# Stream lengths in steps of 16 columns, and a 96-byte shift of the tiles that TensorE streams

## The chip, the core and the metric

The kernel runs on one core of one Trainium2 chip. Its time is the device time of one execution in microseconds (us); of several runs the median is given. The hardware profiler records single executions: for each instruction a start and a duration, for TensorE the clock that it was granted, and for the DMA engines what they moved.

## What is computed

Two steps follow each other. The first is linear attention without a mask, for 8 batches of 8 heads, 576 positions and 64 features:

```python
kv  = einsum('bhsd,bhse->bhde', k, v)
out = einsum('bhsd,bhde->bhse', q, kv)
out = out / sqrt(mean(out * out, axis=-1) + 1e-6) * g_norm
```

Its result is read as 4608 tokens of 512 features. The second step is a mixture of 16 experts in 4 groups of 4. Each token chooses a group and then an expert of that group by the largest logit, is weighted with both softmax values, and passes through that expert alone:

```python
h  = maximum(x_of_expert @ w1[expert], 0)     # 512 -> 1024
ye = h @ w2[expert]                           # 1024 -> 512
out[tokens] = weight[:, None] * ye
```

## The kernel before

**Two stages.** In the first stage (to about 143 us) q, k and v are loaded, the products of attention and the logits of the router are made, and each token gets a place ("slot") in the list of its expert. The scaled rows of the tokens are kept in DRAM. In the second stage the experts are worked through in order of size, largest first, as 16 "regions" r = 0 to 15. The list `CAPS` (line 22) says how many slots a region has; it falls from 384 to 256. A region that had more tokens than slots would leave the rest to a loop at the end of the kernel, whose number of turns is computed on the device. Region 0 is done in the first stage and in the passage between the stages, in plain float32; the change doesn't touch its capacity.

**One region, r = 1 to 14.** The work is split so that float32 accuracy is kept while TensorE works on the type float32r. Each operand is written as a sum of a high and a low part: `xh`, `xl` for the tokens, `hh`, `hl` for the hidden layer, `whi`, `wlo` for the weights. A product is then three matmuls, high by high, low by high and high by low; `three` (lines 305 to 317) issues them, at lines 310, 311 and 315. In all regions but the last TensorE loads a 128 x 128 block of weights (LDWEIGHTS) and streams the tokens against it, so that the number of columns of each stream is the region's capacity:

- layer 1 (`layer1`): 8 blocks of features f, 4 blocks of the inner dimension, 3 matmuls each: 96 matmuls into the PSUM tiles `ps`, from `xh` and `xl`. After each f, ScalarE makes `hh` and VectorE `hl` (`split_h`, lines 284 and 285).
- layer 2 (`layer2_by_feature`): 4 blocks of output features d, 8 inner blocks, 3 matmuls each: 96 matmuls into the PSUM tiles `psy`, from `hh` and `hl`.

So a region is 192 matmuls, and regions 1 to 15 are 2880. Region 15 does its layer 2 the other way round (`layer2_by_token`): there the blocks of `hh` and `hl` are loaded, and 256 columns of `whi` or `wlo` are streamed.

**What runs beside it.** The order of instructions on each engine is the order in which they are written (a manual schedule). While region r is on TensorE, the loop over f issues the gather of the rows of region r + 2 (GpSimd queue, `gather`, line 1230), their scaling on GpSimd (`scale`), their way through DRAM (`put_x`, line 1242, and `get_x`, line 1248, on SyncE's queue), the weight loads of the next regions (line 212) and the scatter of region r - 1's result (`get_y`, `scatter_rows`). During layer 2 the function `side` splits the next region's w1 (lines 245 and 246) and turns and splits its tokens (`turn_x`, line 1253; `split_x`, lines 1262 and 1263). Sizes that go through DRAM in `put_x`, `get_x` and `put_y` are rounded up to 32 rows.

**Where the tiles lie.** Tiles of a pool are placed one behind the other in the order in which they first appear. `whi` and `wlo` are tiles of 8192 bytes per partition in the pool `big`, which lies first. The pool `moe` follows, in the order `xT`, `yq`, `yo3`, `xg`, `xq`, `xt`, the second weight tiles, `xh`, `xl`, `yo`, `hh`, `hl` and small ones. All these tiles but one, up to `hl`, are a multiple of 256 bytes long. The exception is `xg`, the gathered rows: 3 x 520 x 4 = 6240 bytes, which is 24 times 256 and 96 over. A block of weights starts 512 or 1024 bytes behind the last, a chunk of tokens 1536 bytes, so within the tiles nothing changes modulo 256. Modulo 256 bytes, every stream from `xh`, `xl`, `hh` or `hl` therefore starts 96 bytes behind the start of every weight block. In layer 2 of region 15, where the roles are exchanged, that is -96, or 160.

Of the kernel before, what the change touches and what calls it, by code (L numbers as in the profile page):

```python
# [9 lines left out]
F32 = mybir.dt.float32  # L10
# [8 lines left out]

CAPS = [384, 364, 354, 330, 326, 312, 302, 300, 292, 290, 284, 274, 268, 264, 260, 256]


GS = [8, 7, 5, 5, 7, 4]
# [32 lines left out]
def tile_linattn_moe(ctx: ExitStack, tc: tile.TileContext, qm, qt, k, v, router, w1, w2, out):  # L58
    nc = tc.nc
    P = 128  # L60
# [25 lines left out]
    RW = DM + H  # L86
# [70 lines left out]
    for r in range(NE):  # L157
        nc.gpsimd.memset(caps[:, r:r + 1], float(CAPS[r]))
    blk = cp.tile([P, 36], F32, name="blk")
# [88 lines left out]
    def blocks(cap):  # L248
        return [(j, min(P, cap - j * P)) for j in range((cap + P - 1) // P)]

    def gather_rows(xg, rows, idx, src=scr):
        return nc.gpsimd.indirect_dma_start(out=xg[0:rows, 0:RW], out_offset=None, in_=src,  # L252
                                            in_offset=bass.IndirectOffsetOnAxis(ap=idx[0:rows, :], axis=0))
# [20 lines left out]
    def scale_rows(eng, xg, out_=None):  # L274

        x = by_quarter(xg[:, 0:DM])
        out_ = x if out_ is None else by_chunk(out_)
        for h in range(2):
            hs = slice(2 * h, 2 * h + 2)
            d = eng.tensor_tensor(out=out_[:, hs], in0=x[:, hs], in1=factors(xg)[:, h], op=ALU.mult)  # L280
        return d
# [855 lines left out]
    with ExitStack() as ph:  # L1137
        mp = ph.enter_context(tc.tile_pool(name="moe", bufs=2))
# [87 lines left out]
        def quarter_rows(x, cap, a):  # L1226
            n = (cap + 31) // 32
            return x[0:32 * n, a * P:(a + 1) * P].rearrange("(b i) f -> i b f", i=32)

        def gather(r):  # L1230
            xg = mp.tile([P, 3, RW], F32, name="xg", bufs=1)
            for j, _ in blocks(CAPS[r]):
                st["gather"] = gather_rows(xg[:, j], P, gidx[:, r, j:j + 1])
            return xg

        def scale(r, g):
            for j, _ in blocks(CAPS[r]):
                scale_rows(nc.gpsimd, g[:, j])

        def put_x(r, g):  # L1240
            for j, rows in blocks(CAPS[r] + -CAPS[r] % 32):
                nc.sync.dma_start(xd[r % 2][j * P:j * P + rows, :], g[0:rows, j, 0:DM])

        def get_x(r):
            n = (CAPS[r] + 31) // 32
            xq = mp.tile([P, 12, P], F32, name="xq", bufs=1)
            for a in range(4):
                nc.sync.dma_start(xq[32 * a:32 * a + 32, 0:n, :], quarter_rows(xd[r % 2], CAPS[r], a))
            return xq, mp.tile([P, KC, 384], F32, name="xt", bufs=1)
# [80 lines left out]
        for i in range(2):  # L1330
            load_next(i)
        nxt = gather(1)
        gather_rows(xr, P, gidx[:, 0, 2:3])
        scatter_rows(st["ys"][:, 0, :], P, gidx0[:, 0:1])
# [5 lines left out]
        for i in range(2, 4):  # L1340
            load_next(i)
        nxt = gather(2)
        scale(2, nxt)
        left = ps_t.tile([P, 512], F32, name="left", tag="pst")
# [34 lines left out]
        for r in range(1, NE):  # L1379
# [10 lines left out]
            for f in range(FC):  # L1390
                if f in w2_at:
                    split_piece(w2c, w2_at[f], r in MOVED)
                ps = ps_h.tile([P, 512], F32, name="ps")
                layer1(ps[:, 0:cap], w1c, f, xh[:, :, 0:cap], xl[:, :, 0:cap])
                split_h(hh[:, f, 0:cap], hl[:, f, 0:cap], ps[:, 0:cap])
                if r > 1:
                    next(tables, None)
                    next(tables, None)
                elif f < len(psys):
                    nc.vector.memset(psys[f][:, DM // 2:384], 0.0)  # L1400
                if f == 0:
                    nxt2 = gather(r + 2) if r + 2 < NE else None
                if nxt2 and f == 1:
                    scale(r + 2, nxt2)
                if f >= 1:
                    next(turns, None)
                if todo and todo[0] in MOVED and f == 2:
                    results = get_y(*todo)
                if nxt and f in (1, 3):
                    load_next((f + 3) // 2)  # L1410
                if nxt2 and f == 4:
                    put_x(r + 2, nxt2)
                if f >= 5 and results:
                    scatter_rows(*results.pop(0))
                if f == FC - 1 and r + 1 == NE:
                    nc.gpsimd.drain()
# [26 lines left out]
    with ExitStack() as ph:  # L1443
# [4 lines left out]
        with tc.For_i(0, nv, 1) as it:  # L1448
# [19 lines left out]
            xg = op.tile([P, RW], F32, name="xgo")  # L1468
# [90 lines left out]
```

## Time and profile before

| | us |
|---|---|
| median of 3 runs | 572.38 |
| lowest and highest of the runs | 571.86, 573.12 |
| the profiled execution's own time | 569.92 |
| its span, from the first instruction to the last | 568.2 |

Rows of the profile name the line of the kernel, the engine, the operation, the tile written and the tiles read. PE is a matmul on TensorE, PEld the load of its weights, DVE is VectorE, ACT is ScalarE, POOL is GpSimd, SP is SyncE. Matmuls overlap: a matmul's recorded duration is the time from its start until its last column is out, and the next one starts long before that. What a matmul costs in a dense sequence is the time from its start to the next one's start, called its pitch here. A window from the first matmul of a region to the first of the next, divided by 192, is the region's mean pitch.

### The profile page before, as it was taken

The numbers are of one execution on the slowest core, as the hardware profiler recorded it, in microseconds if no ns is written. First come the engines' busy times: TensorE is split into PE (matmuls) and PEld (weight loads), VectorE is DVE, ScalarE is ACT, GpSimd is POOL, SyncE is SP. The second block draws the span as 40 slices with busy tenths as digits, with TensorE's granted clock in tenths as the row PEclk, the third lists the DMA queues.
The fourth block names the chain that finished last, engine by engine and source line by source line (L and its number), as shares of the span: only waits on it lengthen the run. The fifth ranks groups of instructions, "written<-read, shape, count | busy, mean of one in ns | idle before, by whom it ended". The sixth has DMA issues, their size and how long they took to land.

```text
span 568.2 us, 11528 instructions
## 1 busy us (share of the span) xinstructions
PE 545.6 (96%) x4335; PEld 523.7 (92%) x4335; DVE 376.8 (66%) x777; ACT 268.5 (47%) x530; POOL 208.9 (37%) x278
## 2 busy tenths in 40 slices
PE   8999988799989999999999999999999999999995
PEld 4789877588879999999999999999999999999995
DVE  4236988772467686676767676777767677877850
ACT  0367764621444344444545445454546455555540
POOL 4014433143461525152352434343526263630321
PEclk9999998999999999999999999999999999999998
DMA  9999999487979998899988999999999999799730
GB/s 268 371 413 376 365 363 397 153 312 247 276 282 323 281 344 222 262 318 294 303 248 300 260 323 262 316 266 319 299 307 282 300 320 320 273 279 306 253 116 33
DMA packets 77359, 164.06 MB, mean 289 GB/s; under 512 B 7979, under 2 KB 46075, under 8 KB 66293
## 3 DMA queue, kind: packets, MB, share of 16 engines
q1 hardware_dynamic: 69331, 141.14, 77.2%
q0 software_dynamic: 7824, 22.11, 13.2%
q8 instruction: 35, 0.57, 0.4%
q10 hardware_dynamic: 146, 0.04, 0.1%
q14 instruction: 23, 0.19, 0.1%
HBM read 125.82 MB, written 37.96 MB: 288 GB/s over the span
## 4 chain that ended last, share of the span: by engine, by line
PE 77%; DMA 13%; issue 3%; DVE 2%; ACT 2%; POOL 1%; SPq 1%; POOLq 0%; DVEq 0%; ACTq 0%
PE psy L310 11%; PE psy L315 11%; PE psy L311 11%; PE ps L311 11%; PE ps L315 11%; PE ps L310 11%; DMA m_v<-in_v_dram 3%; DMA m_q<-in_qm_dram 3%; PE l L299 3%; DMA m_k<-in_k_dram 3%; PE ops L515 2%; DMA scr<-xo 2%; PE kps L477 2%; PE ps L299 1%; DMA xs<-scr,sidx 1%
## 5 line engine op out<-in xcount | busy, mean ns | idle before, releaser
L246 DVE TENSOR_TENSOR wlo<-wr,whi 128x1024 fp32r<-128x1024 f32 (+1 forms) x172 | 155.2, 928 | 25.1 <-ACT whi L245 22.9
L310 PE MATMUL ps<-xh,whi 128*128 128x364 f32 (+14 forms) x480 | 144.9, 302 | 1.0 <-ACT xh L1262 1.0
L311 PE MATMUL ps<-xl,whi 128*128 128x364 f32 (+14 forms) x480 | 144.8, 302 | 0.4 <-DVE xl L1263 0.4
L315 PE MATMUL ps<-xh,wlo 128*128 128x364 f32 (+14 forms) x480 | 144.4, 301 | 0.0
L311 PE MATMUL psy<-hl,whi 128*128 128x364 f32 (+13 forms) x448 | 135.4, 302 | 0.0
L315 PE MATMUL psy<-hh,wlo 128*128 128x364 f32 (+13 forms) x448 | 135.4, 302 | 0.0
L310 PE MATMUL psy<-hh,whi 128*128 128x364 f32 (+13 forms) x448 | 135.3, 302 | 0.0
L245 ACT CAST whi<-wr 128x1024 fp32r<-128x1024 f32 (+1 forms) x172 | 127.9, 783 | 0.0
L284 ACT ACTIVATE hh<-ps 128x364 fp32r<-128x364 f32 (+14 forms) x120 | 50.5, 421 | 149.6 <-PE ps L315 148.5
L256 POOL DMA_INDIRECT out_dram<-yo,gall x45 | 55.5, 1234 | 110.9 <-DMA yo<-yd 90.4
L285 DVE SCALAR_TENSOR_TENSOR hl<-ps,hh 128x364 fp32r<-128x364 f32 (+14 forms) x120 | 55.9, 466 | 59.5 <-ACT hh L284 59.4
L310 PEld LDWEIGHTS ps<-xh,whi 128*128 128x128 f32 x480 | 90.8, 189 | 1.7 <-ACT xh L1262 1.6
L311 PEld LDWEIGHTS ps<-xl,whi 128*128 128x128 f32 x480 | 90.5, 189 | 1.2 <-DVE xl L1263 1.1
L280 POOL TENSOR_TENSOR xg<-xg 128x256 f32<-128x256 f32 x82 | 61.1, 770 | 80.4 <-DMA xg<-scr,gall 80.4
L315 PEld LDWEIGHTS ps<-xh,wlo 128*128 128x128 f32 x480 | 90.7, 189 | 0.0
L310 PEld LDWEIGHTS psy<-hh,whi 128*128 128x128 f32 x448 | 84.7, 189 | 0.0
L315 PEld LDWEIGHTS psy<-hh,wlo 128*128 128x128 f32 x448 | 84.6, 189 | 0.0
L311 PEld LDWEIGHTS psy<-hl,whi 128*128 128x128 f32 x448 | 84.5, 189 | 0.0
L252 POOL DMA_INDIRECT xg<-scr,gall x44 | 47.5, 1079 | 76.1 <-DMA xd<-xg 60.8
L1262 ACT ACTIVATE xh<-xt,rw 128x364 fp32r<-128x364 f32 (+14 forms) x60 | 32.5, 543 | 45.4 <-DVE xt L1253 45.4
L1315 DVE STREAM_TRANSPOSE yq<-psy 128x320 f32<-128x320 f32 (+3 forms) x52 | 26.7, 514 | 29.9 <-PE psy L315 29.8
L515 PE MATMUL ops<-kvx,m_q 128*128 128x168 f32 x256 | 42.0, 312 | 1.1 <-ACT xr L466 0.6
(254 smaller groups left out, 593.6 us busy)
## 6 DMA issues: line engine op xcount, KB each, us to landing
wr<-in_w_dram SPq DMA_DIRECT2D x64, 1024.0 KB, 9.2
scr<-xo SPq DMA_DIRECT2D x36, 256.0 KB, 9.1
m_q<-in_qm_dram SPq DMA_DIRECT2D x8, 1024.0 KB
xd<-xg SPq DMA_DIRECT2D x32, 256.0 KB, 5.7
m_k<-in_k_dram SPq DMA_DIRECT2D x7, 1024.0 KB, 8.3
m_v<-in_v_dram SPq DMA_DIRECT2D x7, 1024.0 KB
yo<-yd SPq DMA_DIRECT2D x26, 256.0 KB, 3.9
xq<-xd SPq DMA_DIRECT2D x20, 160.0 KB, 8.6
```

What stands on the lines that cost most here:

```text
L245: nc.scalar.copy(out=hi, in_=x)
L246: nc.vector.tensor_tensor(out=lo, in0=x, in1=hi.bitcast(F32), op=ALU.subtract)
L252: return nc.gpsimd.indirect_dma_start(out=xg[0:rows, 0:RW], out_offset=None, in_=src, in_offset=bass.IndirectOffsetOnAxis(ap=idx[0:rows, : ...
L256: sc = nc.gpsimd.indirect_dma_start(out=out, out_offset=bass.IndirectOffsetOnAxis(ap=idx[0:rows, :], axis=0), in_=yo[0:rows, :], in_offset ...
L280: d = eng.tensor_tensor(out=out_[:, hs], in0=x[:, hs], in1=factors(xg)[:, h], op=ALU.mult)
L284: nc.scalar.activation(out=hh, in_=ps, func=AF.Relu)
L285: nc.vector.scalar_tensor_tensor(out=hl, in0=ps, scalar=0.0, in1=hh.bitcast(F32), op0=ALU.max, op1=ALU.subtract)
L310: nc.tensor.matmul(ps, lhsT=stat_h(c), rhs=mov_h(c), start=(c == 0), stop=False)
L311: nc.tensor.matmul(ps, lhsT=stat_h(c), rhs=mov_l(c), start=False, stop=False)
L315: nc.tensor.matmul(ps, lhsT=stat_l(d), rhs=mov_h(d), start=False, stop=(d == n - 1))
L515: nc.tensor.matmul(o, lhsT=raw["q", b].rearrange("p j f -> p (j f)")[:, (pr * NJ + j) * P:(pr * NJ + j + 1) * P], rhs=kvx[b % 4][:, pr], s ...
L1262: nc.scalar.activation(out=xh, in_=x, func=AF.Copy, scale=g2[:, 0:1])
```

## The change

The capacities are raised to the next multiple of 16, and `xg` gets 24 more floats, which nothing reads or writes, so that all tiles behind it move by 96 bytes. The streams then start 192 bytes behind the weight blocks, modulo 256; in layer 2 of region 15 it is 64.

```diff
-CAPS = [384, 364, 354, 330, 326, 312, 302, 300, 292, 290, 284, 274, 268, 264, 260, 256]
+CAPS = [384, 368, 368, 336, 336, 320, 304, 304, 304, 304, 288, 288, 272, 272, 272, 256]
...
         def gather(r):
-            xg = mp.tile([P, 3, RW], F32, name="xg", bufs=1)
+
+
+            xg = mp.tile([P, 3 * RW + 24], F32, name="xg", bufs=1)[:, 0:3 * RW].rearrange("p (j f) -> p j f", j=3)
             for j, _ in blocks(CAPS[r]):
                 st["gather"] = gather_rows(xg[:, j], P, gidx[:, r, j:j + 1])
             return xg
```

## Rows read from the trace of the kernel before

**Rows 1.** The page: busy time, clock in 40 slices, chain that ended last.

```profile
PE 545.6 (96%) x4335; PEld 523.7 (92%) x4335; DVE 376.8 (66%) x777; ACT 268.5 (47%) x530; POOL 208.9 (37%) x278
PEclk9999998999999999999999999999999999999998
PE 77%; DMA 13%; issue 3%; DVE 2%; ACT 2%; POOL 1%; SPq 1%; POOLq 0%; DVEq 0%; ACTq 0%
```

**Rows 2.** Windows of single regions: capacities 364, 354, 302, 300, 292, 290, 268, 264, 260, 256.

```profile
core 0: us, PE busy (x) PEld busy (x) DVE busy (x) ACT busy (x) POOL busy (x), PEclk, DMA share, GB/s
158.92:193.91 34.99, 33.56 (x194) 32.18 (x193) 22.65 (x39) 16.79 (x31) 13.54 (x17) 1.00 0.93 294
193.91:225.90 31.99, 31.99 (x194) 31.99 (x194) 24.75 (x48) 13.70 (x24) 13.44 (x17) 1.00 0.98 291
...
312.19:339.07 26.88, 26.88 (x194) 26.88 (x193) 19.03 (x32) 13.27 (x24) 11.18 (x12) 1.00 1.02 297
339.07:365.94 26.87, 26.87 (x194) 26.87 (x193) 19.00 (x32) 13.22 (x24) 11.58 (x12) 1.00 0.97 293
365.94:391.35 25.41, 25.41 (x195) 25.41 (x193) 18.95 (x32) 13.15 (x24) 10.45 (x11) 1.00 0.98 295
391.35:417.59 26.24, 26.24 (x195) 26.24 (x193) 18.82 (x32) 13.11 (x24) 9.35 (x12) 1.00 1.01 308
...
467.72:492.53 24.81, 24.81 (x206) 24.73 (x205) 19.03 (x35) 14.33 (x27) 11.70 (x12) 1.00 0.91 281
492.53:515.88 23.35, 23.35 (x194) 23.35 (x193) 18.14 (x32) 12.85 (x24) 8.30 (x10) 1.00 0.99 302
515.88:538.92 23.04, 23.04 (x194) 23.04 (x193) 17.57 (x32) 12.73 (x23) 4.23 (x3) 1.00 0.92 289
538.92:561.84 22.92, 22.92 (x194) 22.87 (x192) 8.39 (x13) 7.03 (x14) 4.96 (x5) 1.00 0.28 86
```

**Rows 3.** The same windows with TensorE alone: the sum over regions 1 to 15.

```profile
sum 402.92, PE 401.49; mean PE 26.77
```

**Rows 4.** Timeline of the first matmuls at capacity 302: start us, us, engine, line, operation.

```profile
312.19 0.30 PE L310 MATMUL ps<-xh,whi 128*128 128x302 f32 x1
312.19 0.19 PEld L311 LDWEIGHTS ps<-xl,whi 128*128 128x128 f32 x1
312.33 0.30 PE L311 MATMUL ps<-xl,whi 128*128 128x302 f32 x1
312.33 0.19 PEld L315 LDWEIGHTS ps<-xh,wlo 128*128 128x128 f32 x1
312.47 0.30 PE L315 MATMUL ps<-xh,wlo 128*128 128x302 f32 x1
```

**Rows 5.** Timeline between the stages: 16 plain float32 matmuls of 256 columns, merged.

```profile
139.80 3.62 PE L303 MATMUL left<-wr,h 128*128 128x256 f32 x16
```

**Rows 6.** Matmuls by line and form: busy us, mean duration ns, idle before.

```profile
L310 PE MATMUL psy<-hh,whi 128*128 128x364 f32 x32 | 10.5, 329 | 0.0
...
L310 PE MATMUL psy<-hh,whi 128*128 128x292 f32 x32 | 9.5, 296 | 0.0
L311 PE MATMUL psy<-hl,whi 128*128 128x292 f32 x32 | 9.5, 296 | 0.0
...
L315 PE MATMUL psy<-hh,wlo 128*128 128x292 f32 x32 | 9.3, 292 | 0.0
...
L303 PE MATMUL left<-wr,h 128*128 128x256 f32 x16 | 3.6, 379 | 0.0
```

**Rows 7.** Timeline of VectorE in layer 2 at capacity 264: its last split of tokens.

```profile
513.63 0.45 DVE L1263 SCALAR_TENSOR_TENSOR xl<-xt,rw,xh 128x260 fp32r<-128x260 f32 x1
514.00 1.22 DVE L246 TENSOR_TENSOR wlo<-wr,whi 128x1024 fp32r<-128x1024 f32 x1
```

**Rows 8.** VectorE's split of the hidden layer in the windows of capacities 302 and 264.

```profile
L285 DVE SCALAR_TENSOR_TENSOR hl<-ps,hh 128x302 fp32r<-128x302 f32 x8 | 3.8, 470 | 4.8 <-ACT hh L284 4.8
...
L285 DVE SCALAR_TENSOR_TENSOR hl<-ps,hh 128x264 fp32r<-128x264 f32 x8 | 3.4, 429 | 3.1 <-ACT hh L284 3.1
```

## The prediction

> **What bounds the kernel now.** I first read the page [rows 1]: TensorE is busy for 96% of the span, it makes up 77% of the chain that ended last, and its granted clock is at the upper level (2.4 GHz) in nearly every slice. A busy TensorE need not be one at its peak, so the second view is the table of windows, one per region [rows 2]. From capacity 354 on, TensorE has no idle time in a region, and VectorE is the next at 19 of 27 us. So in this stage the end is set by the pitch of the matmuls, and by nothing that ends a wait. The windows of regions 1 to 15 add up to 402.9 us [rows 3], out of 568.2.
>
> The third step compares the pitch with the columns. In the timeline [rows 4] matmuls of 302 columns start 140 ns apart, and so does the window: 26.88 us / 192 = 140.0. One column per tick of 2.4 GHz would be 302 / 2.4 = 125.8 ns, so 14.2 ns per matmul are something else, called the excess. It isn't a matter of the column count: capacity 290 takes 26.24 us and capacity 292 only 25.41 [rows 2]. Per matmul that is 136.7 and 132.3 ns, an excess of 15.8 and 10.7. Capacity 354 has 166.6 - 147.5 = 19.1, and 302 and 300 take the same time. Nor is it a fixed cost of an instruction: plain float32 matmuls of 256 columns, between the stages, start (3.62 - 0.379) / 15 = 216.1 ns apart [rows 5, 6]; this form takes two ticks per column, 213.3 ns, so its excess is 2.7 ns, although it too loads weights for each matmul.
>
> What goes on during a float32r stream: the weights of the next matmul are loaded, from the same start on, for 190 ns [rows 4]. Stream and load read the same memory side by side, the stream at one word per tick without slack. My reading is that they meet in some part of the memory at times, and that the stream then waits; the half-rate stream has slack and doesn't. Where two address sequences meet depends on their distance and on where each stream begins and ends, which fits an excess that changes with two columns more or less.
>
> **What the change does to TensorE.** It adds columns: the capacities of regions 1 to 15 sum to 4476 before and 4592 after. 116 columns x 192 matmuls / 2.4 GHz = 9.3 us, all on the path, since TensorE is never idle there. This is sure, whatever else happens.
>
> It may remove excess. From the 402.9 us I take the stalls of the first region: its matmuls of 329 ns [rows 6] less 162.4 (the mean duration of the three kinds at capacity 292, 294.7, less its pitch of 132.3) are a pitch of 167, so 192 of them are 32.0 to 32.1 us of the 34.99 [rows 2], and 2.9 are stalls. I also take 1.4 us for the 12 transposes in the window of capacity 268 (206 instructions instead of 194). 398.6 us remain. The columns are 4476 x 192 / 2.4 = 358.1 us, so the excess is 40.5 us, 14.1 ns for each of 2880 matmuls. The change breaks even where the new excess is 14.1 - 9.3 / 2.88 = 10.9 ns.
>
> No row shows a stream of a multiple of 16 columns at a distance of 192 bytes, so I bound it. From below, 2.7 ns, the half-rate stream. From above, 14.1, the present mean, with one row near that: capacity 256 is a multiple of 16, at the old distance of 96 bytes (160 in its layer 2), and has 22.92 / 192 = 119.4 ns, an excess of 12.7 [rows 2]. It shows that a multiple of 16 alone isn't enough. Between them stand the best kinds of matmul that a region has: at capacity 292 the third kind lasts 292 ns where the others last 296 [rows 6], a pitch of 129.6 and an excess of 8. There identical shapes alternate between better and worse meetings, because the stream's end falls on another place each time. With all streams a whole number of 64-byte pieces, starting at a multiple of 64 from the weights, every matmul of all regions would meet its load in the same way. I take this to be a good meeting, and for its excess the middle between the floor (2.7) and the best kind that still has odd ends (8): 5.3 ns. Then regions 1 to 15 take 367.4 + 2880 x 5.3 ns = 382.6 us instead of 398.6, **16.0 us less**.
>
> **What lies beside it.** VectorE and ScalarE work on more columns: (470 - 429) / 38 = 1.1 ns per column in the split of the hidden layer [rows 8], some 0.1 us in a region, and hidden, as VectorE has 5 to 8 us to spare in each [rows 2]. If regions become shorter, the latest thing that TensorE needs is the last `xl`: at capacity 264 it ends at 514.08 [rows 7], 1.8 us before the next region starts at 515.88 [rows 2]; layer 2 would become at most 96 x 5.6 ns = 0.5 us shorter there even at the floor (116.0 against 121.6 ns), so the cover holds. The w1 piece behind it is needed only by the last feature blocks. On the queues nothing moves: rounded up to 32, all capacities give the sizes of before, so `put_x`, `get_x` and `put_y` and the transposes move the same bytes, and the gathers have the same three blocks; `get_y` and the scatters carry 116 rows more in all, off the path. The 24 floats of `xg` are never touched. I cost all of this at nothing. The DMA engines show a busy share near 1 [rows 2]; they move 281 to 308 GB/s in the middle regions, and a region that is 6% shorter would ask for as much more. A load that then comes late is the point where this cover could fail.
>
> **The rivals.**
>
> *The excess goes entirely* (2.7 ns): 367.4 + 7.8 = 375.2 us, 23.4 less, 549.0. For it: the half-rate stream reaches this floor with the same loads beside it. Against it: no float32r row does.
>
> *The meeting is a fixed one, but a bad one.* Today the excess varies and averages out; after the change one relation holds for all 2880 matmuls. Capacities 302 and 260 sit at one pitch, with 14.2 and 120.0 - 108.3 = 11.7 ns [rows 2]. If the new relation is like that of capacity 256, 12.7 ns, the stage takes 367.4 + 36.6 = 404.0 us, 5.4 more: 577.8. It decides from 10.9 ns upwards.
>
> *Addresses don't matter.* If the excess came from issuing or from the array, it would stay at 14.1 ns and only the columns would count: 581.7. Against it stand capacities 290 and 292. The Trainium skill ("SBUF — State Buffer", section "Who interferes with whom") says that TensorE has two independent read ports, one for the moving operand and one for the weights, and never waits on anyone; by that rule the shift can bring nothing and this rival holds. The float32r rows with 10 to 19 ns over one tick per column speak against it, but they don't show the reason.
>
> *The shift isn't where the diff says* (tiles placed in another way), or excess and columns cancel: within 1.1 us of before.
>
> *Another limit takes over*: late weights or rows give back half of the gain, some 564.
>
> **The numbers.** The sum was made on the profiled execution, 569.92 us with a span of 568.2; the median of the runs lies 2.5 higher, at 572.38. I subtract from the median: 572.4 - 16.0 = **556.4 us**. Chances: the forecast with its neighbours (3.5 to 10 ns) 0.45, no excess left 0.23, another limit 0.02, nothing measurable 0.06, bad meeting 0.14, addresses without effect 0.10. So faster by over 0.2% (about what a measurement of this kernel can tell from no change) 0.70, within 0.2% 0.06, slower 0.24. The range goes from the floor, less the scatter of runs, to the bad meeting: 547 to 578; it leaves out the last rival.
>
> **What would show it.** If I am right, the window of capacity 304 is 192 x (126.7 + 5.3) = 25.3 us, three kinds of matmul last alike, and equal capacities (four regions of 304) take equal times. The stage's windows add up to some 387. If the windows of 304 are 26.6 us or more (an excess of 12), the meeting is bad or addresses don't matter; capacity 256, whose columns are unchanged, tells those two apart: its 22.92 us change only if the distance matters. A new idle time of TensorE inside a region, with a DMA or `xl` as its end, would be the other limit.

## The result, and the profile of the changed kernel

The changed kernel takes **576.61 us** (median of 7 runs, 574.99 to 578.31), against 571.60 for the kernel before on the same occasions (7 runs, 568.81 to 573.12): a ratio of 1.0095 [1.007, 1.012], **slower by about 5 us**. The forecast was 556.4; the range, up to 578, holds it. The profiled execution took 574.99 us, 5.07 more than that of before.

The page of the changed kernel, answering to [rows 1]:

```profile
span 573.3 us, 11529 instructions
PE 552.1 (96%) x4335; PEld 529.7 (92%) x4335; DVE 384.3 (67%) x777; ACT 269.6 (47%) x530; POOL 211.8 (37%) x278
PEclk9999998799999999999999999999999999999998
PE 77%; DMA 13%; issue 3%; DVE 2%; ACT 2%; SPq 1%; POOL 1%; POOLq 0%; DVEq 0%; ACTq 0%
```

The same 4335 matmuls, the same share, the same chain: nothing has taken TensorE's place as the bound. The windows, answering to [rows 2, 3], are of regions with capacity 368, 304 (twice), 288, 272 (twice) and 256; the last line sums all 15:

```profile
core 0: us, PE busy (x) PEld busy (x) DVE busy (x) ACT busy (x) POOL busy (x), PEclk, DMA share, GB/s
194.53:226.96 32.43, 32.43 (x194) 32.43 (x193) 25.86 (x48) 13.81 (x24) 16.00 (x18) 1.00 0.95 289
...
340.62:367.25 26.63, 26.63 (x195) 26.63 (x193) 19.41 (x32) 13.27 (x24) 13.96 (x14) 1.00 0.96 298
367.25:393.87 26.62, 26.62 (x195) 26.62 (x193) 19.01 (x32) 13.28 (x24) 9.68 (x11) 1.00 1.02 302
...
420.50:446.09 25.59, 25.59 (x194) 25.59 (x193) 18.73 (x32) 13.02 (x23) 11.23 (x12) 1.00 1.00 313
...
471.69:496.72 25.03, 25.03 (x207) 24.98 (x205) 19.72 (x35) 14.40 (x27) 12.93 (x14) 1.00 0.87 289
496.72:520.40 23.68, 23.68 (x195) 23.68 (x193) 18.38 (x32) 12.96 (x24) 4.86 (x6) 1.00 0.94 294
...
544.08:566.69 22.61, 22.61 (x194) 22.57 (x192) 8.39 (x13) 7.01 (x14) 4.48 (x4) 1.00 0.28 85
sum 407.56, PE 406.10 PEld 404.57 DVE 290.28 ACT 197.19 POOL 156.05; mean PE 27.07 PEld 26.97 DVE 19.35 ACT 13.15 POOL 10.40
```

The stage takes 407.56 - 402.92 = 4.64 us more [rows 3], which is nearly all of the 5.07. The columns alone are worth 9.28, so the change has won back 4.64 elsewhere. Each window over 192 gives the pitch, and that less columns / 2.4 GHz the excess: 168.9 ns and 15.6 at capacity 368, 138.7 and 12.0 at 304, 133.3 and 13.3 at 288, 123.3 and 10.0 at 272, 117.8 and 11.1 at 256. Over all 2880 matmuls, without the first region's stalls (2.97 us; 2.91 before) and the 12 transposes in the window of one of the regions of 272 (1.35 us, as before), the excess is 35.9 us, 12.5 ns for each, where it was 14.1. The forecast wanted 5.3.

The three kinds of matmul last alike now, where [rows 6] had 296, 296 and 292 at capacity 292:

```profile
L315 PE MATMUL psy<-hh,wlo 128*128 128x304 f32 x128 | 38.5, 301 | 0.0
L311 PE MATMUL psy<-hl,whi 128*128 128x304 f32 x128 | 38.5, 301 | 0.0
L310 PE MATMUL psy<-hh,whi 128*128 128x304 f32 x128 | 38.5, 301 | 0.0
```

But that is a mean. The starts in the trace show that single pitches still wander, in a cycle; eleven in a row, in ns:

```
after, capacity 304:   140 136 137 142 139 139 137 136 143 138 139
before, capacity 292:  133 131 133 134 129 133 134 130 133 134 129
```

### The profile page after: what moved, and what is told of

It is laid out like the page before. It is cut to its first block, busy times and chain, and to the rows that moved or that the text cites. A ratio compares the mean times of both kernels' runs of the same rounds, so it can differ in the third digit from the quotient of the medians.

```text
span 573.3 us, 11529 instructions
## 1 busy us (share of the span) xinstructions
PE 552.1 (96%) x4335; PEld 529.7 (92%) x4335; DVE 384.3 (67%) x777; ACT 269.6 (47%) x530; POOL 211.8 (37%) x278
## 4 chain that ended last, share of the span: by engine, by line
PE 77%; DMA 13%; issue 3%; DVE 2%; ACT 2%; SPq 1%; POOL 1%; POOLq 0%; DVEq 0%; ACTq 0%
PE psy L311 11%; PE psy L315 11%; PE psy L310 11%; PE ps L311 11%; PE ps L315 11%; PE ps L310 11%; DMA m_v<-in_v_dram 3%; DMA m_q<-in_qm_dram 3%; PE l L299 3%; DMA m_k<-in_k_dram 2%; PE ops L515 2%; DMA scr<-xo 2%; PE kps L477 2%; PE ps L299 1%; DMA xg<-scr,gall 1%
## 5 line engine op out<-in xcount | busy, mean ns | idle before, releaser
L310 PE MATMUL ps<-xh,whi 128*128 128x304 f32 (+6 forms) x480 | 145.8, 304 | 1.0 <-ACT xh L1264 1.0
L311 PE MATMUL ps<-xl,whi 128*128 128x304 f32 (+6 forms) x480 | 145.6, 303 | 0.4 <-DVE xl L1265 0.4
L315 PE MATMUL ps<-xh,wlo 128*128 128x304 f32 (+6 forms) x480 | 145.2, 303 | 0.0
L311 PE MATMUL psy<-hl,whi 128*128 128x304 f32 (+5 forms) x448 | 136.3, 304 | 0.0
L315 PE MATMUL psy<-hh,wlo 128*128 128x304 f32 (+5 forms) x448 | 136.3, 304 | 0.0
L310 PE MATMUL psy<-hh,whi 128*128 128x304 f32 (+5 forms) x448 | 136.1, 304 | 0.0
L284 ACT ACTIVATE hh<-ps 128x304 fp32r<-128x304 f32 (+6 forms) x120 | 51.2, 427 | 152.5 <-PE ps L315 146.2
L256 POOL DMA_INDIRECT out_dram<-yo,gall x45 | 49.1, 1092 | 130.1 <-DMA yo<-yd 86.0
L285 DVE SCALAR_TENSOR_TENSOR hl<-ps,hh 128x304 fp32r<-128x304 f32 (+6 forms) x120 | 56.9, 474 | 57.8 <-ACT hh L284 55.2
L1264 ACT ACTIVATE xh<-xt,rw 128x304 fp32r<-128x304 f32 (+6 forms) x60 | 32.9, 550 | 45.6 <-DVE xt L1255 44.1
L1317 DVE STREAM_TRANSPOSE yq<-psy 128x320 f32<-128x320 f32 (+3 forms) x52 | 26.6, 512 | 28.7 <-PE psy L315 26.5
```

Source lines behind the costliest of these rows:

```text
L256: sc = nc.gpsimd.indirect_dma_start(out=out, out_offset=bass.IndirectOffsetOnAxis(ap=idx[0:rows, :], axis=0), in_=yo[0:rows, :], in_offset ...
L284: nc.scalar.activation(out=hh, in_=ps, func=AF.Relu)
L285: nc.vector.scalar_tensor_tensor(out=hl, in0=ps, scalar=0.0, in1=hh.bitcast(F32), op0=ALU.max, op1=ALU.subtract)
L310: nc.tensor.matmul(ps, lhsT=stat_h(c), rhs=mov_h(c), start=(c == 0), stop=False)
L311: nc.tensor.matmul(ps, lhsT=stat_h(c), rhs=mov_l(c), start=False, stop=False)
L315: nc.tensor.matmul(ps, lhsT=stat_l(d), rhs=mov_h(d), start=False, stop=(d == n - 1))
```

## The experiments

Theory A: the excess depends on the distance of the stream from the weights, together with the length. Theory B: on the length alone. Theory C: other engines and the DMAs slow the streams. Each excess below is a mean pitch less columns / 2.4 GHz.

**The two halves of the change by themselves.** The capacities without the 24 floats of `xg`, and the 24 floats with the old capacities:

```diff
-CAPS = [384, 364, 354, 330, 326, 312, 302, 300, 292, 290, 284, 274, 268, 264, 260, 256]
+CAPS = [384, 368, 368, 336, 336, 320, 304, 304, 304, 304, 288, 288, 272, 272, 272, 256]
```

> The raised capacities without the shift: streams stay 96 bytes behind the weights. Columns cost 9.3 us. Theory A: the excess differs from that of the whole change (12.3 ns on average), so the time differs from the whole change's 576.6 by more than 2 us either way. Theory B: the time of the whole change, within 1 us, as the shift does nothing.

```diff
-            xg = mp.tile([P, 3, RW], F32, name="xg", bufs=1)
+            xg = mp.tile([P, 3 * RW + 24], F32, name="xg", bufs=1)[:, 0:3 * RW].rearrange("p (j f) -> p j f", j=3)
```

> The shift alone, with the old capacities: streams 192 bytes behind the weights. No column is added. Theory A: windows of the regions change by some per cent, some up, some down; a time between 565 and 580. Theory B: nothing changes, within 1 us of the kernel before, region by region within 0.1 us.

The capacities alone took 581.02 us, a ratio to before of 1.0175 [1.0139, 1.0211]; the shift alone 570.23, 0.9966 [0.9936, 0.9997]. Windows of the capacities alone (one of 336, one of 304, one of 272, and 256):

```profile
227.10:256.55 29.45, 29.45 (x194) 29.45 (x194) 22.99 (x48) 13.60 (x24) 11.58 (x14) 1.00 0.92 287
...
341.35:368.55 27.20, 27.20 (x195) 27.20 (x194) 18.57 (x32) 13.27 (x24) 9.98 (x12) 1.00 0.90 282
...
499.77:524.09 24.32, 24.32 (x194) 24.32 (x193) 18.56 (x33) 12.96 (x24) 5.33 (x7) 1.00 1.01 316
...
548.41:571.19 22.78, 22.78 (x194) 22.73 (x192) 8.39 (x13) 6.99 (x14) 4.62 (x4) 1.00 0.29 85
sum 412.05, PE 410.45 PEld 408.91 DVE 287.41 ACT 197.13 POOL 151.31; mean PE 27.36 PEld 27.26 DVE 19.16 ACT 13.14 POOL 10.09
```

And of the shift alone (capacities 300, 292, 256):

```profile
341.00:367.24 26.24, 26.24 (x194) 26.24 (x193) 19.97 (x32) 13.21 (x24) 11.61 (x12) 1.00 0.99 306
367.24:393.48 26.24, 26.24 (x194) 26.24 (x193) 19.29 (x32) 13.15 (x24) 11.60 (x11) 1.00 1.01 311
...
541.20:562.97 21.77, 21.77 (x194) 21.73 (x192) 8.39 (x13) 7.00 (x14) 4.03 (x4) 1.00 0.29 88
sum 400.80, PE 399.17 PEld 397.58 DVE 289.82 ACT 196.29 POOL 151.73; mean PE 26.61 PEld 26.51 DVE 19.32 ACT 13.09 POOL 10.12
```

So the capacities cost 412.05 - 402.92 = 9.13 us of the stage, what their columns cost in the sum; rounding the lengths by itself wins nothing. This holds for the sum of 15 regions and not for each: the region raised from 330 to 336 columns pays nothing for its six (29.45 us against 29.44), and four columns more, from 268 to 272, take a pitch from 122.2 to 126.7 ns, where they are worth 1.7. The window of 330 before:

```profile
225.90:255.34 29.44, 29.44 (x194) 29.44 (x194) 21.34 (x48) 13.52 (x24) 10.18 (x11) 1.00 0.90 278
```

The whole change is 4.4 us faster than the capacities alone, where theory A wanted more than 2 of difference. The shift wins 2.12 us at the old capacities and 412.05 - 407.56 = 4.49 at the new. It acts on lengths that didn't change, and not always for the better: capacity 300 goes from 26.87 to 26.24, 256 from 22.92 to 21.77, but 292 from 25.41 to 26.24 [rows 2]. That ends theory B.

**A map without the kernel.** The matmuls alone, with nothing beside them, for 21 lengths and the distances 0, 32 and so on to 224 bytes:

```diff
+    for n, d in PAIRS:
+        ps = last = pp.tile([P, 512], F32, name=f"n{n}d{d}", tag="ps")
+        for i in range(37):
+            lo = i // 3 % 4 * 384 + d // 4
+            nc.tensor.matmul(ps[:, 0:n], lhsT=w[:, (i % 8) * P:(i % 8 + 1) * P], rhs=x[:, lo:lo + n], start=(i == 0), stop=(i == 36))
```

> Nothing is left of the kernel but float32r matmuls: for each of 21 stream lengths and 8 distances (0 to 224 bytes in steps of 32) a group of 37 matmuls, each with its load of weights, no other engine at work, no DMA. Theory A (stream and load meet in memory): within one length the pitch changes by several ns with the distance, and at the distances of the kernels it repeats them: 140.0 ns for 300 columns at 96, 166.6 for 354 at 96, 138.7 for 304 at 192, 123.3 for 272 at 192. Theory B (the length alone counts): the same values, but flat over the distance, to 0.5 ns. Theory C (other engines or the DMA slow the stream in the kernel): everywhere columns / 2.4 GHz + about 2.7 ns, so 129.4 for 304 columns.

Timeline of TensorE, all eight distances of one length merged into a row; from one row's start to the next one's, over 296, is the mean pitch of a length:

```profile
238.33 41.28 PE L42 MATMUL n302d<-x,w 128*128 128x302 f32 x296
279.45 41.16 PE L42 MATMUL n300d<-x,w 128*128 128x300 f32 x296
320.45 39.72 PE L42 MATMUL n292d<-x,w 128*128 128x292 f32 x296
360.01 40.12 PE L42 MATMUL n290d<-x,w 128*128 128x290 f32 x296
399.97 39.05 PE L42 MATMUL n284d<-x,w 128*128 128x284 f32 x296
...
714.94 43.58 PE L42 MATMUL n320d<-x,w 128*128 128x320 f32 x296
758.37 41.42 PE L42 MATMUL n304d<-x,w 128*128 128x304 f32 x296
799.62 39.52 PE L42 MATMUL n288d<-x,w 128*128 128x288 f32 x296
838.98 37.35 PE L42 MATMUL n272d<-x,w 128*128 128x272 f32 x296
```

That is a mean excess of 13.1 ns at 302, 13.5 at 300, 12.0 at 292 and 14.2 at 290, against 13.4 at 320, 12.7 at 304 and 13.0 at 288. **In the mean, multiples of 16 are no better.** By distance (mean of the 32 pitches from the 5th matmul of a group on; ns of excess):

```
length    0 B   32 B   64 B   96 B  128 B  160 B  192 B  224 B
 256     13.2   11.1   11.1   13.0   12.1   10.7    6.7   11.7
 272     12.2   12.5   13.3   13.3   13.2   11.0   10.0   13.3
 292     11.7   11.7   10.3   10.7   10.0   13.8   15.0   11.7
 300     14.8   13.4   13.0   15.0   13.7   13.3   11.7   13.5
 304     11.2   13.3   11.0   14.9   13.2   13.4   11.9   13.3
 320     13.3   13.3   13.4   13.3   13.3   13.3   13.3   13.3
 354     12.5   12.5   12.6   19.2   15.8   12.5   19.0   14.2
```

The column of 96 bytes repeats the kernel before: 13.0, 10.7, 15.0 and 19.2 at 256 (layer 1), 292, 300 and 354, where it had 13.3, 10.6, 15.0 and 19.2. Over all 15 lengths 13 come back within 0.3 ns; 284 (12.6, in the kernel 15.0) and 312 (15.0, in the kernel 14.4) don't. The column of 192 gives 11.9 and 10.0 for the 12.0 and 10.0 of the changed kernel at 304 and 272, but not its 13.3 at 336 (map 15.9) or its 11.1 at 256 (map 6.7). With no other engine at work the excess is there, so as its source theory C is out.

The excess hides a regularity of the pitch itself. Of the map's 167 mean pitches (without 364 at 0 bytes, the first group, which began with pitches of 302 ns) 71 lie within 0.1 ns of a multiple of 16 ticks of 2.4 GHz, that is of 6.67 ns: 120.0, 126.7, 133.3, 140.0, 146.7, 153.3 and so on; evenly spread pitches would give 5. So different lengths share a pitch, as 300 and 302 or 330 and 336 do at 96 bytes. At multiples of 16 columns the commonest excess is 13.3 ns, which is the columns and 32 ticks: 31 of their 56 pairs have it, and 8 of the other 111.

**Which part of the load matters.** Groups of 61 matmuls: parts of the weights, both operands moved together, other types:

```diff
+            nc.tensor.matmul(ps[0:m, 0:n], lhsT=ww[0:kk, wo:wo + m], rhs=xx[0:kk, lo:lo + n], start=(i == 0), stop=(i == 60))
```

> Again matmuls alone, 61 per group. Theory A: with weight blocks of 64 or 32 columns instead of 128 the load is shorter and meets the stream less, so the excess at 304, 300 and 354 columns falls to about a half and a quarter; moving stream and weights together by 32 to 192 bytes changes nothing; bfloat16 at full rate has a small excess, about 2.7 ns; plain float32 (two ticks per column) about 2.7 ns too; longer streams (384 to 512 columns) keep an excess of some 10 to 19 ns, since there is one load per stream whatever its length. Theory B: the excess doesn't change with the columns of the weight block, and follows the length in some pattern. If the excess is a share of the stream's own time, it grows with the length: at 512 columns by 512/304 = 1.7 against 304.

TensorE's timeline for 304 columns at 192 bytes, with 128 and with 32 weight columns, then with both operands moved by 192 bytes, then in bfloat16 and in plain float32 (two records for a matmul):

```profile
213.81 8.62 PE L56 MATMUL cols128d192n<-x,w 128*128 128x304 f32 x61
...
267.59 8.69 PE L56 MATMUL cols32d192n<-x,w 128*32 128x304 f32 x61
...
390.11 8.63 PE L56 MATMUL base192d192n<-x,w 128*128 128x304 f32 x61
...
407.11 8.05 PE L56 MATMUL bf304d<-xb,wb 128*128 128x304 bf16 x61
...
422.78 31.38 PE L56 MATMUL full304d<-raw,wf 128*128 128x304 f32 x122
```

The loads of the same groups (busy us, mean ns of one):

```profile
L56 PEld LDWEIGHTS <-wb 128*128 128x128 bf16 x122 | 11.9, 98 | 3.8
L56 PEld LDWEIGHTS cols128d192n<-x,w 128*128 128x128 f32 x61 | 8.5, 188 | 0.0
...
L56 PEld LDWEIGHTS cols32d192n<-x,w 128*32 128x32 f32 x61 | 6.6, 108 | 2.0
```

Starts from the 7th matmul on give these excesses in ns (plain float32: per record). With all columns and rows 354 at 96 bytes has 15.8 here and 19.2 in the map, so that its column can't tell an effect of the parts from a second value of the same pair:

```
                                    304 at 192 B   300 at 96 B   354 at 96 B
128 weight columns, 128 rows             12.0          15.0          15.8
 64 weight columns                       13.3          12.8          14.7
 32 weight columns                       13.3          11.7          19.2
 64 rows                                 12.0          15.0          19.2
both moved by 32, 64, 128, 192 B         12.0          15.0
bfloat16                                  2.5           2.5
plain float32                             2.5
```

The distance counts, not where the pair lies: for both pairs tried, moving both operands changes nothing. A load of 108 ns instead of 188 leaves an excess of the same size, so the load's length isn't what is paid: theory A's half and quarter didn't come. The other account put down there, that the excess is a share of the stream's own time, does better: 512 columns have 20.0 ns at 192 bytes, 1.67 times the 12.0 of 304 (1.7 were expected), and 20.2 at 96, though 1.35 times the 15.0. In the map's means over the distances it goes from 11.2 at 256 to 15.0 at 368, 10.5 and 9.8% of the stream's time. No run streams without loading weights, so that the load is what delays the stream isn't shown. The two types with a small excess are those that stream half the bytes per ns: bfloat16 with 2 bytes a column, and plain float32 with two ticks a column.

**A finer map, and the partner changed.** The odd multiples of 16 bytes, and pairs of the first map with the weights moved in place of the stream ("moved"), one block of weights for all matmuls ("one"), or two PSUM banks by turns ("turns"):

```diff
+            wo = (i % 8 * many) * P + (64 - s // 4 if s else 0)
+            nc.tensor.matmul(pss[i % banks][:, 0:n], lhsT=w[:, wo:wo + P], rhs=x[:, lo:lo + n], start=(i < banks), stop=(i >= 37 - banks))
```

> This kernel leaves out all of the computation; it only streams. Groups of 37 float32r matmuls without gaps: the 15 old lengths at the eight distances 16, 48, ... 240 bytes that the first map left out, and some pairs of the map again. Theory A (the excess of a pitch over columns / 2.4 GHz is set by length and distance together): the pairs done again give the first map's value within 0.3 ns (354 at 96: 19.2; 326 at 32: 10.8; 312 at 128: 10.4; 292 at 128: 10.0; 256 at 192: 6.7); the same distance made by moving the weights and not the stream gives the same (300 at 96: 15.0; 304 at 192: 12.0). The finer distances lie between 6 and 20 ns and some lengths have a better place there. Theory B (length alone): all distances of a length within 0.5 ns. On what meets the stream: if it is the load of other weights, the groups that load the same weights each time ('one') or that write two banks by turns ('turns') fall to the 2.5 ns that bf16 showed; if it is the load as such or the stream alone, they stay at 15.0 (300 at 96) and 12.0 (304 at 192).

```
           first map    again   moved    one   turns
300 at  96    15.0        -      15.0   15.0   15.0
304 at 192    11.9        -      12.0   12.0   12.1
312 at 128    10.4      10.3     10.4   10.4   10.4
256 at 192     6.7      11.1      6.7    6.7    6.7
326 at  32    10.8      14.2
354 at  96    19.2      19.2
```

Moving the weights does what moving the stream does, so it is the relation of the two that acts, as theory A has it. That the same block is loaded again and again changes nothing, and neither do two PSUM banks. Of the pairs done again five can be compared (292 at 128 bytes, not in the table, has 10.0 both times; 364 at 0 stood first in the first map), and two of them came out at another mean pitch, another cadence as it is called from here: theory A's "within 0.3 ns" was too strict. A pair can have more than one cadence. The finer steps found better places for some lengths: 8.4 ns for 300 at 80 bytes and for 284 at 176, 10.6 for 364 at 48.

**Each region at its best and at its worst place.** Old capacities; `xg` 40 floats longer, and the tokens and the hidden layer of region r start at a column of their tiles that sets the distance:

```diff
+XCOL = [0, 16, 0, 48, 8, 32, 40, 56, 32, 0, 8, 32, 16, 0, 0, 48]
...
-            x, xh, xl = (y[:, c, 0:CAPS[r]] for y in [xt] + parts)
+            x = xt[:, c, 0:CAPS[r]]
+            xh, xl = (y[:, c, XCOL[r]:XCOL[r] + CAPS[r]] for y in parts)
```

> The kernel before with its old capacities; each region's split tokens and hidden rows start at a column of their tiles such that the distance is the one at which the first map had the least excess for that length (64, 0, 192, 32, 128, 160, 224, 128, 0, 32, 128, 64, 0, 0, 192 bytes for 364 to 256). The map's excess over the 15 regions of 192 matmuls is 31.7 us, against 40.4 at the 96 bytes of before. Theory A (length and distance together): 8.7 us less, 563.2 us against 571.9. Theory B (length alone): 571.9, no change. Theory C (other engines' work sets the pitches of the whole kernel): under half of it, 568 or more.

> The same kernel with each region at the distance where the first map had the most excess (32, 96, 0, 160, 96, 64, 0, 192, 160, 160, 0, 160, 128, 128, 0 bytes): 43.7 us of excess against 40.4. Theory A: 3.2 us more than before, 575.1 us, and 12 us more than the kernel with the best places, though both issue the same instructions. Theory B: 571.9 and equal to the kernel with the best places. Theory C: the two differ by under 6 us.

Best places: 564.90 us, **0.9880 [0.9854, 0.9905]**. Worst places: 571.77, 1.0006 [0.9980, 1.0033]. Windows of 354, 330 and 302 columns at the best places:

```profile
196.18:226.91 30.73, 30.73 (x194) 30.73 (x194) 25.08 (x48) 13.70 (x24) 13.91 (x17) 1.00 0.97 303
226.91:256.67 29.76, 29.76 (x194) 29.76 (x194) 21.59 (x48) 13.53 (x24) 9.85 (x11) 1.00 0.90 277
...
311.72:337.96 26.24, 26.24 (x194) 26.24 (x193) 18.87 (x32) 13.26 (x24) 10.64 (x11) 1.00 0.96 298
...
sum 396.92, PE 395.03 PEld 393.48 DVE 285.67 ACT 196.11 POOL 152.26; mean PE 26.34 PEld 26.23 DVE 19.04 ACT 13.07 POOL 10.15
```

And at the worst places (354, 302):

```profile
195.21:227.21 32.00, 32.00 (x194) 32.00 (x193) 26.68 (x48) 13.69 (x24) 16.42 (x18) 1.00 0.93 292
...
313.28:338.90 25.62, 25.62 (x195) 25.62 (x194) 18.50 (x32) 13.24 (x24) 8.70 (x8) 1.00 1.04 313
...
sum 403.31, PE 401.86 PEld 400.33 DVE 287.26 ACT 195.89 POOL 155.41; mean PE 26.79 PEld 26.69 DVE 19.15 ACT 13.06 POOL 10.36
```

The same instructions on the same columns differ by 403.31 - 396.92 = 6.39 us with their places, and by 6.9 us in the timed runs: theory A, at somewhat over half of the 12 us that the map gave. Theory C's "under 6 us" is missed only narrowly, and the "worst" places are no worse than the kernel before, where theory A wanted 3.2 us. What is missing is in regions that took another cadence than the map's: 330 at 192 bytes has 17.5 ns (map 11.4; the next expectation calls it 12.5, the map's value at 160), and at the "worst" places 302 has 25.62 / 192 = 133.4 ns, an excess of 7.6 (map 14.2).

**The finer places, and the change's capacities at their best.**

```diff
-XCOL = [0, 16, 0, 48, 8, 32, 40, 56, 32, 0, 8, 32, 16, 0, 0, 48]
+XCOL = [0, 12, 12, 4, 8, 32, 40, 20, 32, 28, 44, 32, 60, 0, 36, 4]
```

> The kernel before with its old capacities, each region at the distance with the least excess in both maps, those in steps of 16 bytes too (48, 48, 16, 32, 128, 160, 80, 128, 112, 176, 128, 240, 0, 144, 16 bytes for 364 to 256). The maps' sum is 29.6 us of excess, against 40.4 at the 96 bytes of before. Theory A2 (a pair of length and distance has one cadence, or one of two or three, and keeps the one that it starts in): 10.8 us less than before, 560.5 us, up to 564 where some regions take a longer cadence of theirs (as 330 columns at 192 bytes did: 12.5 ns in the map, 17.5 in the kernel). Rival B2 (the excess is a property of the length, and the gain of the first set of places was the luck of one program): 568 to 572.

```diff
+CAPS = [384, 368, 368, 336, 336, 320, 304, 304, 304, 304, 288, 288, 272, 272, 272, 256]
+XCOL = [0, 0, 0, 0, 0, 0, 12, 12, 12, 12, 0, 0, 48, 48, 48, 4]
```

> The change's capacities, each region at its best distance in the maps (0 bytes for 368 to 320, 48 for 304, 0 for 288, 192 for 272, 16 for 256). Theory A2 (lengths that are multiples of 16 are as any others, and cost their columns): 32.0 us of excess against the 35.8 that the changed kernel's trace shows, 572.8 us: no faster than the kernel before, since the 9.3 us of columns stay. Rival (the prediction's: multiples of 16 can meet their loads well, and the change only missed the distance): 5.3 ns a matmul, 15.3 us of excess, 556.

The finer places took 564.35 us, 0.9881 [0.9856, 0.9905], which timing can't tell from the first set; both beat the kernel before and the changed one. Capacity 300 and the sum:

```profile
335.72:361.34 25.62, 25.62 (x194) 25.62 (x193) 19.25 (x32) 13.21 (x24) 10.64 (x11) 1.00 1.01 316
...
sum 394.39, PE 392.64 PEld 391.10 DVE 285.59 ACT 196.08 POOL 157.26; mean PE 26.18 PEld 26.07 DVE 19.04 ACT 13.07 POOL 10.48
```

The stage is 8.5 us shorter than before in this profile (the map said 10.8), and the median stands just past the long end of what was expected, 564. The change's capacities at their best places took 576.12 us, 1.0059 [1.0032, 1.0085], 3.3 us more than the 572.8 expected, not clearly better than the changed kernel, and far from the 556 of the prediction's idea (capacity 304 and the sum):

```profile
341.35:368.23 26.88, 26.88 (x195) 26.88 (x193) 19.65 (x32) 13.28 (x24) 10.87 (x12) 1.00 0.93 293
...
sum 407.61, PE 405.96 PEld 404.41 DVE 288.37 ACT 197.42 POOL 146.01; mean PE 27.06 PEld 26.96 DVE 19.22 ACT 13.16 POOL 9.73
```

The four regions of 304 at 48 bytes took 13.3 ns each, where the measurement by itself had 10.0, which alone is 2.6 us: one more pair with two cadences.

**Chance or program.** Three of these kernels once more, unchanged, for a second profile:

> The kernel with the worst places once more, for a second profile of the same program. Its first one had 302 columns at 64 bytes at an excess of 7.5 ns (14.2 in the map) and 326 at 160 bytes at 14.2 (17.5 in the map). If the cadence of a pair is fixed by the program (what ran before it, in which order): the same 15 pitches within 0.1 ns. If it is chance at the start of a region: some of these two, or of 354, 256 and 330, come out at another of their values, by 1.5 ns or more.

> The kernel with the finer places once more. Its first profile had 284 at 176 bytes at 11.7 ns (8.4 in the map), 354 at 48 bytes at 14.2 (12.5 in the map) and 256 at 16 bytes at 10.0 and 13.3 (6.7 in the map). Cadence fixed by the program: the same pitches within 0.1 ns. Cadence by chance at the start: one or more of these differ by 1.5 ns or more, and the span differs by 192 times that for each.

> The kernel with the change's capacities at their best places once more. Its first profile had all four regions of 304 columns at 48 bytes at 13.3 ns, where the map had 10.0. Cadence fixed by the program: the four at 13.3 again. By chance: some of them at 10.0, and its time, 576.0 in the first profile, lower by 0.64 us for each.

In the first, all 15 pitches came back within 0.1 ns, 302 at 7.5 included; in the third the four regions of 304 again had 13.3. In the second, 13 regions came back and two didn't: 264 at 0 bytes went from 10.0 to 11.3, and 256, in its layer 2, from 13.3 to 10.7. So the cadence is mostly set by the program and only in few regions by the run.

In the region of 264 the trace shows where it turned. Its first nine pitches go 122, 122, 116 ns, a mean of 120.0 as in the first profile; then TensorE waits for the last `xl`, and from there to the end of the region it runs a longer cycle, with 11.3 ns of excess:

```profile
489.10 0.19 PEld L313 LDWEIGHTS ps<-xl,whi 128*128 128x128 f32 x1 [0.45 <-DVE xl L1266]
```

So here the change of cadence came with an interruption of TensorE. In region 15, of 256, TensorE has no idle time, and its layer 2 changed all the same.

## Why the prediction was wrong

**Right: the bound and the columns.** TensorE's pitch sets the stage before and after; nearly all of the stage's 4.64 us is pitch. "This is sure, whatever else happens" was said of the columns' 9.3 us, and the capacities alone show 9.13 in the stage, as a sum; region by region the added columns cost nothing or more than their time.

**Right: the work beside it at nothing.** The stalls of the first region are 2.97 us against 2.91, the window with the transposes holds the same 1.35 us, and no other window has idle time of TensorE. What the prediction took for the latest thing needed, the last `xl`, came late once, by 0.45 us at capacity 264, in one of the two profiles of the finer places.

**Right in kind: the excess depends on where stream and weights lie.** The shift alone shows it, and so do the best and the worst places.

**Wrong: "every matmul of all regions would meet its load in the same way. I take this to be a good meeting, and for its excess the middle between the floor (2.7) and the best kind that still has odd ends (8): 5.3 ns."** This is the step that failed, in both halves. Not in the same way: the excess of the changed kernel runs from 10.0 ns at 272 to 15.6 at 368, and single pitches of 304 from 136 to 143. Not a good one: 12.5 ns in the mean. The term of -16.0 us is therefore 9.28 - 4.64 = +4.64. The premise, that whole 64-byte pieces meet their loads in one way and well, is what the map denies: over eight distances 304, 288 and 320 have 13.0 ns of excess on average, 302, 300 and 292 have 12.9. Where multiples of 16 do agree, it is on 13.3 ns.

Both ends of the interpolation were badly chosen. The floor came from a form that streams at half the rate; the parts measured later show 2.5 ns for it and for bfloat16 alike, and no float32r pair under 6.6. The 8 ns were one place in a cycle of three (133, 134 and 130 ns in the series above), whose neighbours pay for it; only the cycle's mean is a pitch. The one row like the changed kernel's, capacity 256 with 12.7 ns [rows 2], was used as the bound from above, and taken as the estimate it would have given 577.8, 1.2 us from the result; in part by luck, since the same 256 columns have between 6.6 and 13.2 ns in the maps, by distance.

**The rivals.** *The meeting is a fixed one, but a bad one* had this time, and a price of 12.7 ns for what came out as 12.5, but not one relation for all matmuls: 5 of the 15 regions (336 twice, 320, 288 twice) share 13.3 ns, the others have 10.0 to 15.6. *The excess goes entirely* is out. *Addresses don't matter* gave 581.7, and the capacities alone, at the old distance, cost about that (581.02), because their mean excess, 14.0 ns, came out as before while single regions went up and down by up to 4.4; with the shift it is 5.1 us too long, and the shift alone moved capacity 256 by 1.15 us. By the Trainium skill ("SBUF — State Buffer", section "Who interferes with whom") TensorE's two read ports are independent and it never waits. By that rule the shift, and the step from the worst to the best places, are worth nothing; the runs show 2.1 and 6.4 us of the stage for them. They don't show where stream and load meet.

**The signs named beforehand** were right but weak: 26.6 us or more at 304 was to mean a bad meeting or addresses without effect, and it is 26.63; 256 was to change only if the distance matters, and went from 22.92 to 22.61, but to 22.78 with the capacities alone, where its distance stayed. Only the shift alone, with 21.77, made this sign clear.

**What stays open.** Whether it is the load that the stream meets, and what in it: the places of both act together, but the load's number of columns or rows doesn't set the size, nor whether the block is new, and the excess grows with the stream. And what sets which of its cadences a pair takes, apart from the one seen to turn at a wait: of 120 regions in eight kernels 94 are within 0.3 ns of a value that the bare loops had for the pair, the others took another.

## What to carry to other kernels

In these runs a dense sequence of float32r matmuls of 240 to 512 columns paid 7 to 20 ns over one column per tick for each matmul, by a relation of length and distance that no rounding rule foretells; measure the few pairs at hand in a bare loop, and then in the kernel, since the loop's value held in about four regions of five. Don't raise stream lengths in the hope that round numbers run better: over 15 regions the added columns were paid in full, though a single region can get some for nothing. When an unmeasured cost is put between two bounds, stay by the row that is most like the new case, not by one of another type.

## What the runs showed of the hardware that was not expected

- A weight load shortened from 188 to 108 ns (32 columns instead of 128) doesn't lower the excess of the stream beside it: 13.3 ns at 304 columns where the full load has 12.0, and 11.7 at 300 where it has 15.0.
- At 320 columns all eight distances give the same excess, 13.3 ns; at 354 they go from 12.5 to 19.2.
- The same pair can run in different cadences: 302 columns at 64 bytes with 14.2 ns in the map and 7.5 in a kernel, in both of that kernel's profiles. 256 at 192 bytes has 6.7 or 11.1.
- Short streams have a floor: 192 and 128 columns of float32r both have a pitch of 111.7 ns at 96 bytes.
- Mean pitches gather at multiples of 16 ticks (6.67 ns): 71 of 167 in the map, where an even spread would give 5.
